# Seventy matmuls of zeros in the first chunks' TensorE waits, and a new order of the first list of steps

## The chip, the cores and the metric

The kernel runs on one core of one Trainium2 chip. The metric is the device time in microseconds (us) of one execution. TensorE multiplies matrices into PSUM, which has eight banks; VectorE (DVE), ScalarE (ACT) and GpSimd (POOL) do the elementwise work; SyncE (SP) issues all DMA transfers of this kernel. Each engine and the SP queue works through its own instructions in order and waits on semaphores for the others.

## The reference

Pooled attention, then two MLPs on its output (shapes: 4 batches, 8 heads, 576 tokens, head size 64; d_model 512; d_ff 1536 and 2048):

```python
k_p = k.reshape(B, H, Sp, 8, D).mean(axis=3)      # v_p likewise
scores = scale * np.matmul(q, k_p.transpose(0, 1, 3, 2))
attn = softmax(scores)                            # rows, with 1e-9 in the sum
x = heads_joined(np.matmul(attn, v_p))            # 2304 x 512
xn = x / sqrt(mean(x * x) + 1e-6) * rms_g
x = (silu(xn @ w_gate) * (xn @ w_val)) @ w_out    # first MLP
h = x @ w_in2
return silu(h) @ w_out2                           # second MLP
```

The MLPs' weights are float64 words in memory; the kernel converts them to float32 by integer operations on both halves of a word, and splits each float32 number into a high and a low part, so that three fast matmuls stand for one exact one.

## The kernel before, in words

The 2304 tokens are eight chunks of 288; two chunks make a batch of the attention. Everything the kernel does is cut into steps, and four long lists written out by hand (`start`, `pair`, `last`, `second`) say in which order the steps are issued. `play` reads a list: a token such as `1x0` means the next step of work `x` number 0 of chunk 1, and a suffix such as `:g` puts that step's free operation on POOL (`:v` on DVE, `:a` on ACT). Since every engine is in order, the list fixes the order on each engine; steps of different engines that stand beside each other in it don't hinder one another.

The steps that the change and the prediction touch, all from the first 60 us:

- `K`, `V`, `Q`: loads of a block of k, v or q (SP). The blocks of k and v first go to early slots, later to rotating buffers; the q blocks of chunks 1 and up share two buffers (`q_load`, lines 299 to 309), so 1Q3 has to wait until a block of chunk 1 was used by its scores.
- `B n`: one of 36 weight blocks, seven steps: load (SP), shift (DVE), scale (ACT), sign (ACT, or DVE with `:v`), join (DVE), high part (ACT), low part (POOL). Blocks 0, 1, 2 are gate, val and out number 0, blocks 3, 4, 5 number 1, and so on (`w_block`, line 207).
- `k j`: the sum over eight keys (DVE), then two copies into `kbd`, a block-diagonal tile whose other half stays zero (`k_sum`, line 331). `a i` and `d i` do the same for v into `vbd0` and `vr0`.
- `m j`: the scores of one pair of heads, three matmuls on TensorE, six records in the profile (line 405). `s j`: the negated maximum (DVE, line 416), then six exponentials with their sums and a scaling (ACT, line 423). `w j`: the reciprocal (DVE), the weighting (DVE or POOL) and a copy of the remaining columns to `rest`.
- `p i`: three transposes on TensorE (line 456) and a copy out of PSUM. `x j`: the product with v on TensorE (lines 490, 491, called `pv`), its square (ACT, line 498), its scaled copy to `xraw`, and, for chunk 0, the sums of squares as matmuls with one column (line 509, `x0.3` is the fourth step of x0).
- `r`, `n`: the root mean square, its broadcast by matmuls (`rs`, line 542) and its use. `y j`: the split of x into `xT`. `Z`: a store of x.
- `G f`, `H f`, `D f`: the gate, val and out matmuls of the first MLP for a chunk and a slice of d_ff, twelve matmuls each (lines 257 to 259).

Chunk 0's attention takes its PSUM banks from a rotation (`att_bank`, line 313) over the tags up (two banks), acc0 to acc3 and att (two banks); chunk 1 and later ones take att alone. A bank is taken again only when the engines that read it are done. The banks acc0 to acc3 hold the out sums of the first MLP from D0 on.

`setup` (line 99) and a memset of `kbd` (line 1065) run ahead of the lists. The tile `early_x` has 1024 columns, of which the first 864 are used.

Of the kernel before, what the change touches and what calls it, by code (L numbers as in the profile page):

```python
# [9 lines left out]
F32 = mybir.dt.float32  # L10
# [12 lines left out]
def tile_pooled_attention_then_two_mlps(  # L23
# [16 lines left out]
    nc = tc.nc  # L40
# [8 lines left out]
    P = 128  # L49
# [3 lines left out]
    CH = S // 2  # L53
# [45 lines left out]
    def setup():  # L99
        make_identity(nc, ident)  # L100
        nc.gpsimd.memset(ones, 1.0)
        nc.gpsimd.memset(mhalf, -0.5)

        nc.vector.tensor_reduce(
            out=mask, in_=ident.rearrange("p (q h r) -> p h q r", h=4, r=REST), axis=AX.XY, op=ALU.add
        )

        nc.gpsimd.memset(vbd0, 0.0)
        for e in range(2):
            nc.vector.tensor_copy(out=vbd[:, e], in_=kbd.rearrange("p j r -> p (j r)")[:, :NPAIR * P])  # L110
# [8 lines left out]
    def ring(dtype, name, n):  # L119
        return w_pools[n < NRING // 2].tile([P, 1024], dtype, tag="w", bufs=NRING // 2, name=name)  # L120
# [5 lines left out]
    early_x = ring(F32, "early_x", next(n_early))  # L126
    early_v = ring(F32, "early_v", next(n_early))
# [183 lines left out]
    banks = ["up", "up", "acc0", "acc1", "acc2", "acc3", "att", "att"]  # L311

    def att_bank(c, name):

        tag = "att"
        if c == 0:
            tag = banks.pop(0)
            banks.append(tag)
        return psum.tile([P, 512], F32, tag=tag, bufs=1 if tag.startswith("acc") else 2, name=name)

# [524 lines left out]
    x2 = {}  # L845
# [148 lines left out]
    def down2(c, m):  # L994
# [70 lines left out]
    nc.vector.memset(kbd, 0.0)  # L1065
# [41 lines left out]
    )  # L1107
    pair = (
# [246 lines left out]
```

## Time and profile before

| what | value |
|---|---|
| median of three runs | 922.28 us (917.54 to 922.48) |
| the profiled execution | 922.12 us, span 920.3 us |
| busy share of the span | PE 98%, DVE 69%, ACT 59%, POOL 41% |
| mean granted clock of TensorE | 0.981 of 2.4 GHz |
| the chain that ended last | PE 81%, DVE 9%, DMA 4%, POOL 3% |

The page of a profile gives shares and groups, the windows give busy times of a stretch, the timeline single instructions. Times count from the start of the span. PE is TensorE, PEld its weight loads. The granted clock is a share of 2.4 GHz and has two levels, 1.00 and 0.50. Matmuls overlap in the records, so their pace is read from the start of one to the start of the next rather than from their length. A wait is put down to the engine whose signal came last.

### The profile page before, as it was taken

The numbers are of one execution on the slowest core, as the hardware profiler recorded it, in microseconds if no ns is written. First come the engines' busy times: TensorE is split into PE (matmuls) and PEld (weight loads), VectorE is DVE, ScalarE is ACT, GpSimd is POOL, SyncE is SP. The second block draws the span as 40 slices with busy tenths as digits, with TensorE's granted clock in tenths as the row PEclk, the third lists the DMA queues.
The fourth block names the chain that finished last, engine by engine and source line by source line (L and its number), as shares of the span: only waits on it lengthen the run. The fifth ranks groups of instructions, "written<-read, shape, count | busy, mean of one in ns | idle before, by whom it ended". The sixth has DMA issues, their size and how long they took to land.

```text
span 920.3 us, 17356 instructions
## 1 busy us (share of the span) xinstructions
PE 901.8 (98%) x6122; PEld 875.4 (95%) x6122; DVE 631.2 (69%) x1254; ACT 542.5 (59%) x1453; POOL 375.8 (41%) x487
## 2 busy tenths in 40 slices
PE   5999999999999999999999999999999999999998
PEld 4689999999999999999999998999999999999998
DVE  6789988765554835443368779658986579766675
ACT  5688887364254714345444546677666677576653
POOL 6435443344215621200027746881038910388200
PEclk8589999999999999999999999999999999999999
DMA  8645642342215321244367885266862668614486
GB/s 281 204 140 174 218 134 64 120 152 78 62 41 134 116 66 40 84 137 144 131 230 258 291 280 182 89 206 206 269 213 63 213 187 264 233 49 161 125 263 208
DMA packets 85259, 149.79 MB, mean 163 GB/s; under 512 B 8627, under 2 KB 53812, under 8 KB 85172
## 3 DMA queue, kind: packets, MB, share of 16 engines
q1 hardware_dynamic: 85172, 148.68, 50.0%
q8 instruction: 48, 0.79, 0.4%
q14 instruction: 39, 0.32, 0.1%
HBM read 116.21 MB, written 32.44 MB: 162 GB/s over the span
## 4 chain that ended last, share of the span: by engine, by line
PE 81%; DVE 9%; DMA 4%; POOL 3%; issue 2%; ACT 1%; SPq 0%; ACTq 0%; POOLq 0%; DVEq 0%
PE P L773 38%; PE pv L257 4%; PE pv L259 4%; PE pv L258 4%; PE pg L258 4%; PE pg L257 4%; PE pg L259 4%; PE acc L258 4%; PE acc L257 4%; PE acc L259 4%; PE sc L405 2%; PE pT L456 1%; PE pv L491 1%; DMA out<-out2s 1%; DMA xw_raw<-xw 1%
## 5 line engine op out<-in xcount | busy, mean ns | idle before, releaser
L773 PE MATMUL P<-xP,in 128*128 128x384 f32 x1008 | 179.5, 338 | 0.7 <-POOL in L244 0.5
L773 PEld LDWEIGHTS P<-xP,in 128*128 128x128 f32 x1008 | 177.5, 188 | 1.6 <-POOL in L244 0.8
L773 PE MATMUL P<-out,hc 128*128 128x256 f32 x1512 | 172.7, 276 | 0.0
L773 PEld LDWEIGHTS P<-out,hc 128*128 128x128 f32 x1512 | 172.5, 188 | 0.0
L244 POOL TENSOR_TENSOR in<-in,in 128x256 fp32r<-128x256 f32 x96 | 78.8, 830 | 112.1 <-ACT in L237 64.5
L237 ACT ACTIVATE hc<-h 128x384 fp32r<-128x384 f32 x144 | 74.1, 525 | 41.8 <-PE P L773 37.7
L244 DVE TENSOR_TENSOR hc<-h,hc 128x384 fp32r<-128x384 f32 x144 | 81.6, 590 | 19.6 <-ACT hc L237 17.7
L257 PE MATMUL pg<-xT,w_gate 128*128 128x288 f32 x240 | 73.0, 304 | 0.8 <-DVE hT L244 0.8
L257 PE MATMUL pv<-xT,w_val 128*128 128x288 f32 x240 | 73.0, 304 | 0.1
L257 PE MATMUL acc<-hT,w_out 128*128 128x288 f32 x240 | 72.4, 302 | 0.0
L258 PE MATMUL pg<-xT,w_gate 128*128 128x288 f32 x240 | 71.6, 298 | 0.2
L258 PE MATMUL acc<-hT,w_out 128*128 128x288 f32 x240 | 71.2, 297 | 0.2 <-DVE hT L244 0.2
L259 PE MATMUL pg<-xT,w_gate 128*128 128x288 f32 x240 | 71.2, 297 | 0.0
L259 PE MATMUL pv<-xT,w_val 128*128 128x288 f32 x240 | 70.9, 295 | 0.0
L258 PE MATMUL pv<-xT,w_val 128*128 128x288 f32 x240 | 70.8, 295 | 0.0
L259 PE MATMUL acc<-hT,w_out 128*128 128x288 f32 x240 | 70.8, 295 | 0.0
L423 ACT ACTIVATE pr<-sc,mx 96x72 f32<-96x72 f32 x192 | 57.9, 314 | 17.8 <-DVE mx L416 17.8
L624 ACT ACTIVATE th<-pg 128x288 f32<-128x288 f32 x57 | 23.5, 413 | 72.1 <-PE pg L259 71.9
L244 POOL TENSOR_TENSOR in<-sums,in 128x256 fp32r<-128x256 f32 x72 | 59.0, 829 | 2.4 <-ACT in L237 2.0
L626 DVE SCALAR_TENSOR_TENSOR th<-th,pg 128x288 f32<-128x288 f32 x57 | 25.6, 448 | 40.1 <-ACT th L624 40.0
L257 PEld LDWEIGHTS pg<-xT,w_gate 128*128 128x128 f32 x240 | 45.7, 190 | 1.3 <-issue 1.0
L258 PEld LDWEIGHTS pg<-xT,w_gate 128*128 128x128 f32 x240 | 45.6, 190 | 0.6 <-DVE xT L244 0.6
(233 smaller groups left out, 2304.4 us busy)
## 6 DMA issues: line engine op xcount, KB each, us to landing
out<-out SPq DMA_DIRECT2D x84, 512.0 KB, 4.7
out<-out2s SPq DMA_DIRECT2D x56, 256.0 KB, 4.1
in<-in SPq DMA_DIRECT2D x24, 512.0 KB, 3.6
raw<-in_moe_w_out_dram SPq DMA_DIRECT2D x18, 512.0 KB, 4.5
raw<-in_moe_w_in_dram SPq DMA_DIRECT2D x16, 512.0 KB, 3.7
early_raw<-in_moe_w_gate_dram SPq DMA_DIRECT2D x10, 512.0 KB, 4.2
early_raw<-in_moe_w_val_dram SPq DMA_DIRECT2D x10, 512.0 KB, 4.9
early_raw<-in_moe_w_out_dram SPq DMA_DIRECT2D x10, 512.0 KB, 4.8
```

What stands on the lines that cost most here:

```text
L237: nc.scalar.activation(out=out, in_=in_, func=AF.Copy, scale=1.0 if scale is None else scale)
L244: ENGINES[engine[0] or usual].tensor_tensor(out=out, in0=in0, in1=in1, op=op)
L257: nc.tensor.matmul(ps, lhsT=whi, rhs=xhi, start=first, stop=False)
L258: nc.tensor.matmul(ps, lhsT=whi, rhs=xlo, start=False, stop=False)
L259: nc.tensor.matmul(ps, lhsT=wlo, rhs=xhi, start=False, stop=last)
L405: nc.tensor.matmul(ps[:TT, a * 2 * SP:(a + 1) * 2 * SP], lhsT=qT[:, a * TT:(a + 1) * TT], rhs=kbd[:, j, :], start=True, stop=True,)
L423: nc.scalar.activation(out=pr[:, a, e], in_=s4[:, a, e], func=AF.Exp, bias=mx[:, a, e:e + 1], accum_out=sm[:, a, e],)
L456: nc.tensor.transpose(ps[:n, a * TT:(a + 1) * TT], src, ident[:TT, :TT])
L491: nc.tensor.matmul(ps, lhsT=vr0[:RR, j, :], rhs=pT_t[c, NPAIR + j // 2], start=False, stop=True)
L624: nc.scalar.activation(out=th, in_=pg, func=AF.Tanh, scale=0.5)
L626: nc.vector.scalar_tensor_tensor(out=th, in0=th, scalar=1.0, in1=pg, op0=ALU.add, op1=ALU.mult)
L773: nc.tensor.matmul(ps, lhsT=a, rhs=b, start=first and n == 0, stop=n == 2, skip_group_check=True)
```

## The change

A step `T` (`warm`) is added to the lists' vocabulary: one float32 matmul of a 128x128 block of zeros with itself, into a PSUM tile `idle` that nobody reads. The zeros are columns of `early_x` that were free; DVE sets them first of all in `setup`, ahead of `kbd`. `idle` takes the bank acc3, so chunk 0's rotation has seven banks instead of eight.

```diff
     def setup():
+        nc.vector.memset(zero, 0.0)
+        nc.vector.memset(kbd, 0.0)
         make_identity(nc, ident)
...
     early_x = ring(F32, "early_x", next(n_early))
+    zero = early_x[:, 3 * CH:3 * CH + P]
...
-    banks = ["up", "up", "acc0", "acc1", "acc2", "acc3", "att", "att"]
+    banks = ["up", "up", "acc0", "acc1", "acc2", "att", "att"]
...
+    idle = []
+
+    def warm(n):
+
+        if not idle:
+            idle.append(psum.tile([P, 512], F32, tag="acc3", bufs=1, name="idle"))
+        nc.tensor.matmul(idle[0][:, :P], lhsT=zero, rhs=zero, start=True, stop=True, skip_group_check=True)
+        yield
...
-    nc.vector.memset(kbd, 0.0)
     setup()
...
     start = (
-        "B0 K1 Q1 K0 k1 Q0 V4 V5 k1:g k0 K2 m1 k0:g 1Q0 1Q1 K3 a5 s1 a4:v V0 m0 Q2 B0 B0 s1 V3 d4:g Q3 B0:v g0 "
-        "1m1 B1 B2 1m0 k2 k2:g s0 s0 1Q2 w1 B0 1s1 w1:g d5:g w1:g a0:v a0:g m2 1s1 w0 p1 k3 w0:g p0 s2 s2 1w1 "
...
+        "K1 T13 T12 T11 T10 T9 T8 T7 T6 T5 Q1 K0 k1 B0 V4 V5 Q0 k1:g k0 K2 T4 m1 T3 T2 T1 T0 T56 1Q1 k0:g T55 s1 "
+        "1Q0 K3 m0 a5 V0 Q2 B0 B0 s1 V3 a4:v d4:g Q3 B0:v T54 T53 1m1 B1 1m0 k2 k2:g s0 s0 w1 w1:g 1Q2 B0 1s1 "
...
-             "X": x2_steps, "O": turn, "g": lambda n: g_load()}
+             "X": x2_steps, "O": turn, "g": lambda n: g_load(), "T": warm}
```

All seventy T steps are in `start`. Read from the two lists, TensorE's order up to G1 becomes (Tn is n fillers in a row; x0.3 is the squares' sum of x0; r0 is the broadcast `rs`):

```
before: m1 m0 1m1 1m0 m2 p1 p0 m3 p4 1p1 p2 x0 1m2 1p0 x1 1m3 x0.3 p3 p5 1p4 x3 x2 1x1
        x3.3 x1.3 2m0 1p3 x2.3 1x0 1p5 G0 1p2 r0 1x2 1x3 H0 2p0 G1
after:  T10 m1 T6 m0 T2 1m1 1m0 T5 m2 p1 T7 m3 p0 T8 1p1 T2 p4 p2 1m2 T6 x0 1p0 x1 x0.3 p3
        1m3 T3 p5 T6 1p4 T5 x3 x2 1x1 x3.3 x1.3 2m0 1p3 x2.3 T7 1x0 1p5 G0 1p2 r0 T3 1x3
        1x2 H0 2p0 G1
```

The loads begin with B0 K1 Q1 K0 Q0 V4 V5 before and K1 Q1 K0 B0 V4 V5 Q0 after; later B4 2K0 B3 V2 1Q3 2K1 becomes V2 2K0 B4 1Q3 B3 2K1. On POOL the order w1 d5 w1 a0 w0 k3 becomes w1 w0 w1 k3 d5 (then, behind two more steps, a0). On DVE the work up to G0 is nearly the same: B7's shift moves ahead of it, two steps of B8 and B4 behind it. `pair`, `last` and `second` hold the same steps as before in an order changed in many places, mostly by one to three places on an engine; of the wide gates 8G9 moves back by 21 places on TensorE and 9G5 forward by 11. Two operations change their engine: the high part of B27 (ACT to DVE) and a copy of 6w2 (DVE to POOL).

## Rows read from the trace of the kernel before

**Rows 1.** The page, parts 1 and 2: busy time, then the span in 40 slices.

```profile
PE 901.8 (98%) x6122; PEld 875.4 (95%) x6122; DVE 631.2 (69%) x1254; ACT 542.5 (59%) x1453; POOL 375.8 (41%) x487
...
PEclk8589999999999999999999999999999999999999
...
GB/s 281 204 140 174 218 134 64 120 152 78 62 41 134 116 66 40 84 137 144 131 230 258 291 280 182 89 206 206 269 213 63 213 187 264 233 49 161 125 263 208
```

**Rows 2.** Windows: length; PE, PEld, DVE, ACT, POOL busy (count); clock; DMA share; GB/s.

```profile
13.40:16.80 3.40, 1.44 (x9) 1.02 (x9) 3.10 (x6) 3.37 (x23) 3.12 (x8) 1.00 1.05 381
16.80:21.60 4.80, 2.98 (x12) 2.21 (x12) 2.59 (x9) 4.71 (x30) 4.55 (x6) 0.50 0.79 268
21.60:48.50 26.90, 26.85 (x90) 17.61 (x91) 20.06 (x43) 17.80 (x77) 13.74 (x20) 0.50 0.56 177
48.50:51.20 2.70, 2.70 (x14) 2.70 (x13) 1.61 (x4) 2.52 (x5) 0.66 (x1) 0.55 0.06 25
```

**Rows 3.** Timeline of TensorE: start, length, line, operation, operands, count, idle before, releaser.

```profile
7.26 3.19 PE L405 MATMUL sc<-kbd,early 128*96 128x144 f32 x12 [7.26 <-POOL kbd L241]
...
14.45 0.98 PE L405 MATMUL sc<-kbd,early 128*96 128x144 f32 x6 [1.12 <-POOL kbd L241]
...
17.63 0.74 PE L456 MATMUL pT<-ident,pr 96*128 96x96 f32 x3 [1.72 <-POOL pr L244]
18.87 1.75 PE L405 MATMUL sc<-kbd,early 128*96 128x144 f32 x6 [0.50 <-POOL kbd L241]
...
21.65 1.22 PE L456 MATMUL pT<-ident,pr 96*128 96x96 f32 x6 [0.54 <-DVE early_pT L239]
```

**Rows 4.** Windows: the stretch with the low clock and the one behind it.

```profile
10.00:60.00 50.00, 46.11 (x195) 33.68 (x195) 38.38 (x84) 37.58 (x161) 26.55 (x40) 0.66 0.60 195
60.00:120.00 60.00, 58.79 (x436) 56.31 (x435) 58.73 (x133) 51.20 (x155) 30.62 (x39) 1.00 0.62 195
```

**Rows 5.** Timeline of TensorE again, around and behind the clock's rise.

```profile
35.81 1.33 PE L490 MATMUL pv<-early_pT,early_v 128*128 128x288 f32 x2
...
38.33 1.33 PE L490 MATMUL pv<-pT,early_v 128*128 128x288 f32 x2
...
45.66 1.31 PE L490 MATMUL pv<-pT,early_v 128*128 128x288 f32 x2
...
51.52 0.83 PE L542 MATMUL rs<-ident,ms 96*128 96x96 f32 x6
52.24 0.75 PE L490 MATMUL pv<-pT,early_v 128*128 128x288 f32 x2
...
53.60 0.75 PE L490 MATMUL pv<-pT,early_v 128*128 128x288 f32 x2
...
58.54 0.90 PE L405 MATMUL sc<-kbd,qT 128*96 128x144 f32 x6
59.27 0.59 PE L528 MATMUL ms<-ones,sq 128*96 128x1 f32 x6
```

**Rows 6.** Timeline of DVE: its first instruction.

```profile
0.91 0.54 DVE L1065 MEMSET kbd<- 128x576 f32 x1 [0.91 <-PEq L1339]
```

**Rows 7.** The chain that ended last, its first steps: start, length, what.

```profile
1.22 4.26 DMA early<-in_k_dram
...
6.35 0.40 POOL kbd L241
```

**Rows 8.** Timeline of the SP queue: DMA issues.

```profile
0.72 0.45 SPq L155 DMA_DIRECT2D early_raw<-in_moe_w_gate_dram  x1
...
15.24 0.50 SPq L283 DMA_DIRECT2D kv<-in_v_dram  x1
26.85 0.33 SPq L307 DMA_DIRECT2D qT<-in_q_dram  x1
```

**Rows 9.** Timeline of ACT: first exponentials of two successive readings.

```profile
13.07 0.32 ACT L423 ACTIVATE pr<-sc,mx 96x72 f32<-96x72 f32 x1 [1.23 <-DVE mx L416]
...
15.12 0.30 ACT L423 ACTIVATE pr<-sc,mx 96x72 f32<-96x72 f32 x1
```

328 rows, old and new, of tables (last, pair, second, start) are left out of this document.

## The prediction

> **What bounds the kernel now.** I read the page's busy shares first: TensorE (PE) is busy for 98% of the span, so only what shortens PE's own work or its waits can shorten the run, and the PEclk row has a dip to 5 tenths in its second slice [rows 1]. The windows cut where the clock changes show what that dip is: from 16.8 us to about 51 the granted clock is 0.50, which is 1.2 GHz, and elsewhere 1.00, which is 2.4 GHz [rows 1, 2]. Two things are to be seen there. First, between 21.6 and 48.5 PE is busy for 26.85 of 26.90 us, so at half clock PE itself is the bound; no engine beside it is over 75% busy. Secondly, a busy PE was not enough to bring the clock back. It fell after 13.4 to 16.8, in which PE worked only 1.44 of 3.40 us, and rose within 48.5 to 51.2, when the dense `pg` matmuls of G0 came; between them stand short scores, transposes and the 32-row `pv` products.
>
> The PE timeline adds something that the clock rows hide [rows 3]. Twelve score records take 3.19 us at 7.26, or 0.266 each, and six take 1.75 at 18.87, under a recorded clock of 0.50; but six take 0.98 at 14.45. So the first scores also ran at 1.2 GHz, although the windows print no fall there: the dense scores from 7.26 to 13.33 lifted the clock, and the gaps behind them lost it. The same rows give the gaps: 7.26 before the first score, then 1.12, 1.72, 0.50 and 0.54, for POOL's and DVE's operands.
>
> After 60 us things are different: PE 58.79 and DVE 58.73 of 60 us [rows 4]. There DVE is as full as PE, so time won earlier stays won only if DVE arrives earlier by as much. From 10 to 60 DVE is busy for 38.38 of 50, so it has 11.6 us of idle time to give.
>
> **What a filler costs.** Each T step is one fp32 matmul, 128x128 by 128 columns, in two records as the other fp32 matmuls have. None is in the trace, so bounds from start to start at full clock: the `rs` records (weights 128 columns wide, 96 moving) come every 0.72/6 = 0.12 us, so 0.24 a filler; the scores every 0.73/6 = 0.122 for 144 columns, by columns 0.22 a filler; the `pv` products every 1.36/4 = 0.34 for 288 columns, by columns 0.30 a filler [rows 5]. I take 0.24, since `rs` has the same weights and nearly the same length; both ends stay for the range.
>
> **The change part by part.** All is counted against the `rs` products behind G0, at 51.52 [rows 5], since the order behind them is nearly the same.
>
> 1. Ten fillers ahead of the first score. They need only the small memset of `zero`, which now runs ahead of the 0.54 us memset of `kbd` [rows 6], so PE can begin at about 1.1 us. At half clock (0.48 each) they end at 5.9. The first score is late today because of k1: its load takes 4.26 us from 1.22 on, and DVE's sum and POOL's two copies, the first at 6.35, follow it [rows 7]. In the new list K1 takes B0's place at the head of SP, 0.5 us earlier (0.72 against 1.22) [rows 7, 8], and B0's 512 KB no longer run ahead of it, 1.9 us at the 281 GB/s of the first slice [rows 1]. So k1 is earlier by 0.5 to 1.9 us, and the fillers let the score start no earlier than 5.9: between -0.5 and -1.4, taken as **-1.4**, since the load is nearer to its bytes than to its place in the queue. B0 moves behind K1, Q1 and K0; its first step on DVE stands behind the first maximum, which hides it.
>
> 2. The clock. Work at 1.2 GHz today is 6.1 us of scores (7.26 to 13.33) and 16.8 to 51.0 less 1.9 of gaps, 32.3: together 38.4. At 2.4 GHz a score goes from 1.75 to 0.90 and a `pv` product from 2.52 to 1.36 start to start [rows 3, 5], a factor near 0.53, so the gain is 38.4 x 0.47 = **-18.0** if the clock is held from the first score on.
>
> 3. The gaps of 1.12, 1.72, 0.50 and 0.54 [rows 3] become room for fillers: **-3.9**, to be set against the next item.
>
> 4. The fillers between the first score and G0 are 57: 6, 2, 5, 7, 8, 2, 6, 3, 6, 5, 7 in their groups. 57 x 0.24 = **+13.7** (12.5 to 17.1). Three more ahead of 1x3 add **+0.7**.
>
> 5. New waits: **+2.9** (0 to 5). Chunk 0 now rotates over seven PSUM banks, not eight, so p0 takes a bank of the pair "att" that chunk 1 shares, and 1p1, 1m3, 1p4 and 1x0 each wait until ACT has read the scores in the bank they need. One such reading, of six exponentials and their sums, holds ACT from 13.07 to 15.12, 2.05 us [rows 9]. ACT has nine of these before 1x0, 18.5 us, with copies and conversions between them, and with PE at double speed it has few gaps left. Following the new order by hand with the row durations, these four wait about 0.7, 0.9, 1.0 and 0.3. DVE and POOL queue behind: s3, 1s3 and 2s0 on DVE can't start before their scores.
>
> 6. The SP queue gains, with nothing added. Today the load 1Q3 blocks SP from 15.7 to 26.85, because its buffer is freed by the scores 1m2, at the end of that wait [rows 8]; everything behind it (2K1, B6, 2K3, B7) waits. In the new list 1m2 stands ahead of x0 and comes some 5 us earlier, and V2, 2K0 and B4 are ahead of 1Q3. Only B3 falls behind 1Q3; with 1m2 at 21 its data land near 25.5, where DVE asks for them. I count this at nothing: it keeps DVE's input ahead of a faster PE, and costs about as much as PE would win if it failed (rival 1).
>
> 7. The rest. On PE no step of the first list moves by more than three places among the real steps. In the other lists a few wide gates move further (8G9 by 21), where PE has no idle time. B27's copy goes from ACT to DVE and one copy of 6w2 from DVE to POOL, each under 1 us and far from G0. I take 0, between -2 and +2.
>
> Sum: -1.4 - 18.0 - 3.9 + 13.7 + 0.7 + 2.9 = -6.0. The profiled execution took 922.12 against a span of 920.3 and a median of 922.28 in the runs, so 922.12 - 6.0 = **916.1**, span and what lies around it alike.
>
> **A rule to weigh.** In 21.6 to 48.5 PE had no gaps and stayed at 1.2 GHz [rows 2]. The Trainium skill, in "TensorE: Matmul & The Clock Gate", section "Why this matters for your kernels", says that keeping TensorE continuously busy releases the clock; the rows here disagree, since busy time of this kind did not. By that rule the fillers would matter only in the gaps. The same page, Part 4 on transposes, says that transposes don't count as busy in the same way; that fits the stretch, and makes rivals 2 and 3 possible.
>
> **The rivals.**
> 1. *The other engines become the bound.* With PE twice as fast, the stretch is a chain of maximum (DVE), exponentials (ACT), weighting (POOL, DVE), transposes and copies. For it: ACT and DVE are 75 to 77% busy in 10 to 60 [rows 4]. Against it: a gain of 6 needs half of DVE's 11.6 idle. New waits of 5 rather than 2.9, with fillers at 0.30 each (+3.4), leave a gain of 0.5; half of both leaves 3.3, 918.8. Taken at 919.
> 2. *The clock is lifted but lost again* in the one long stretch without fillers, x3 to x2's square sums. It is 9.85 us today from x2's product at 35.81 to 45.66, and 2.5 more with x3's [rows 5], so 12.4 at half and 6.5 at full clock: losing it gives back about 5.8. That is 922, no change. For it: exactly this work left the clock low. Against it: at full clock `rs` and two `pv` products in a row left it up, since the second came 1.36 behind the first and the scores at 58.54 again took 0.90 [rows 5].
> 3. *Zeros don't count, and the run is slower.* If the clock takes no notice of matmuls of zeros, PE stays at half clock to G0, and 57 fillers at 0.48 are 27.4 us, of which 3.9 fall into gaps, and 1.4 come back from the earlier start; the last three cost 1.4: +23.5, which is 945 (21 to 31 more with fillers at twice 0.22 and twice 0.30). It decides at one point: whether the clock stands at 1.00 when x0 comes. Against it: the scores lifted the clock at about 13 us, although half of their moving operand `kbd` is zeros. The same page of the Trainium skill (Part 1) says that all-zero operands don't trip the current limiter, so one throttle there does see the data; no run here shows that for this one.
> 4. *The later lists cost more than they bring* (item 7, or DVE full from 60 us on): 924 to 926.
>
> **How the numbers follow.** Forecast 0.58, rival 1 0.17, rival 2 0.12, rival 3 0.08, rival 4 0.05. The low end is fillers at 0.22 and no new waits, some 10 us, so 911 with a us for item 7; the high end takes in rivals 1 and 2: 922. Outside it are rivals 3 and 4 and small tails, 0.2 in all. With 0.5% (4.6 us, about what a measurement of this kernel can tell from no change), faster is the forecast, 0.58; same is rival 1 and most of rival 2, 0.27; slower is rivals 3 and 4 and the rest of 2, 0.15.
>
> **What would show it.** The clock at 1.00 from about 7 us through 44; six score records in 0.9 us from the second score on; fillers 0.24 apart; the `rs` products near 44.8 (51.52 before); ACT or DVE named in the waits ahead of 1p1, 1m3 and 1p4; 1Q3 issued near 21; and the same lead of about 6 us still there at 120 and at the end. Wrong would be: a clock of 0.50 anywhere from 15 to 44 for more than a few us (rivals 2, 3), PE gaps of over 5 us in sum before G0 (rival 1), or a lead that shrinks from G0 to the end (rival 4).

## The result, and the profile after

The changed kernel takes 910.33 us (median; 908.33 to 911.95), the kernel before beside it on the same chip 922.38: a ratio of 0.9878, with a 95% interval of 0.9856 to 0.990. In a second comparison it took 911.21 against 921.72 (0.9885, 0.987 to 0.990). The forecast was 916.1 and the range 911 to 922: the direction and the mechanism came out, the gain is twice the forecast, and the first median lies 0.7 us below the range. The profiled execution took 909.87 with a span of 908.1.

The page of the changed kernel, parts 1 and 2, beside [rows 1]:

```profile
PE 899.4 (99%) x6262; PEld 882.0 (97%) x6262; DVE 628.3 (69%) x1255; ACT 540.0 (59%) x1452; POOL 382.7 (42%) x488
...
PEclk9999999999999999999999999999999999999999
```

TensorE has 140 records more (70 fillers of two) and is busy 2.4 us less, since the dip to 5 tenths in the second slice is gone. The windows of the changed kernel, cut where its clock changes, then the two stretches of [rows 4] (columns as in [rows 2]):

```profile
6.48:26.96 20.48, 18.82 (x147) 16.41 (x146) 17.01 (x34) 16.89 (x95) 17.75 (x26) 1.00 0.88 282
26.96:30.37 3.41, 3.41 (x18) 3.33 (x17) 2.63 (x8) 2.33 (x11) 3.35 (x5) 0.50 0.85 249
30.37:42.56 12.19, 12.19 (x85) 9.10 (x85) 10.54 (x23) 9.35 (x40) 5.69 (x10) 1.00 0.83 260
10.00:60.00 50.00, 49.12 (x348) 41.71 (x347) 44.28 (x96) 42.13 (x187) 32.65 (x45) 0.97 0.72 228
60.00:120.00 60.00, 59.58 (x452) 58.55 (x452) 57.84 (x133) 52.03 (x148) 31.97 (x39) 1.00 0.65 211
```

From 6.48 us on the clock stands at 2.4 GHz but for 3.41 us, where it was at 1.2 GHz for 34 us before. DVE, 38.38 of 50 us busy in [rows 4], is now at 44.28: it does the same work in a shorter stage. The timeline of TensorE in the changed kernel, against [rows 3] and [rows 5] (L330 is the filler, L417 the scores, L554 `rs`):

```profile
1.03 4.63 PE L330 MATMUL idle<-early_x 128*128 128x128 f32 x20 [1.03 <-DVE early_x L100]
5.46 1.40 PE L417 MATMUL sc<-kbd,early 128*96 128x144 f32 x6
6.70 1.50 PE L330 MATMUL idle<-early_x 128*128 128x128 f32 x12
9.32 0.95 PE L417 MATMUL sc<-kbd,early 128*96 128x144 f32 x6 [1.11 <-DMA early<-in_q_dram]
...
13.83 0.98 PE L417 MATMUL sc<-kbd,early 128*96 128x144 f32 x6 [0.54 <-POOL kbd L244]
...
17.85 1.98 PE L330 MATMUL idle<-early_x 128*128 128x128 f32 x16
19.67 0.41 PE L468 MATMUL pT<-ident,pr 96*128 96x96 f32 x3
...
26.88 1.56 PE L417 MATMUL sc<-kbd,qT 128*96 128x144 f32 x6
...
44.49 0.83 PE L554 MATMUL rs<-ident,ms 96*128 96x96 f32 x6
```

The first score starts at 5.46 (7.26 before). Ten fillers take 4.43 us at half clock, 0.443 each; eight take 17.85 to 19.67 at full clock, 0.2275 each. No gap stands at 1p1, 1m3, 1p4 or 1x0, where I expected waits for a bank. `rs` starts at 44.49, 7.03 ahead of its 51.52 before.

Below, the lead of a step is its start in the trace of before less its start in the other trace (e1 to e11 are the runs of the sections that follow). What matters is where it grows:

| lead, us | before starts | changed | e1 | e2 | e3 | e4 | e11 |
|---|---|---|---|---|---|---|---|
| `rs` behind G0 | 51.52 | 7.0 | 8.4 | 0.4 | 1.0 | 1.5 | 7.6 |
| H0 | 54.96 | 6.5 | 7.8 | -0.2 | 0.6 | 0.6 | 7.0 |
| first gate of chunk 2 (2G0) | 109.67 | 7.6 | 8.9 | -0.1 | 1.5 | 1.4 | 8.1 |
| first gate of chunk 6 (6G0) | 357.7 | 8.8 | 9.6 | 0.1 | 2.7 | 1.4 | 8.5 |
| first wide product (aW0) | 625.0 | 11.7 | 8.6 | 3.8 | 5.5 | 1.3 | 12.3 |
| last product (cW55) | 915.4 | 12.3 | 8.6 | 3.8 | 5.6 | 1.3 | 12.6 |

So 7 of the 12 us come from the first 45, as the steps of the prediction had it (6.7), and 5 more behind them, where I had put nothing. Each column is one execution. In e12, another execution of the changed kernel, the lead was 5.7 at `rs`, 5.2 at H0 and 11.1 at the last product: the first stage differs by 1.3 us, the growth behind H0 is the same (5.9, and 5.8 above).

### The profile page after: what moved, and what is told of

The parts are those of the page before. It is cut to its first block, busy times and chain, and to the rows that moved or that the text cites. A ratio compares the mean times of both kernels' runs of the same rounds, so it can differ in the third digit from the quotient of the medians.

```text
span 908.1 us, 17610 instructions
## 1 busy us (share of the span) xinstructions
PE 899.4 (99%) x6262; PEld 882.0 (97%) x6262; DVE 628.3 (69%) x1255; ACT 540.0 (59%) x1452; POOL 382.7 (42%) x488
## 4 chain that ended last, share of the span: by engine, by line
PE 87%; DVE 5%; DMA 4%; ACT 2%; issue 1%; POOL 1%; SPq 1%; ACTq 0%; DVEq 0%; POOLq 0%
PE P L785 38%; PE pv L260 5%; PE pv L261 5%; PE pv L262 5%; PE pg L260 5%; PE acc L260 4%; PE acc L261 4%; PE pg L261 4%; PE pg L262 4%; PE acc L262 4%; PE sc L417 2%; DMA out<-out2s 2%; PE pT L468 1%; PE idle L330 1%; DMA early<-in_v_dram 1%
## 5 line engine op out<-in xcount | busy, mean ns | idle before, releaser
L262 PEld LDWEIGHTS pv<-xT,w_val 128*128 128x128 f32 x240 | 45.3, 189 | 0.6 <-POOL w_val L247 0.6
L260 PEld LDWEIGHTS pv<-xT,w_val 128*128 128x128 f32 x240 | 45.1, 188 | 0.7 <-ACT kbd L240 0.4
```

Of the source, the lines that this page charges most:

```text
L260: nc.tensor.matmul(ps, lhsT=whi, rhs=xhi, start=first, stop=False)
L262: nc.tensor.matmul(ps, lhsT=wlo, rhs=xhi, start=False, stop=last)
```

## Which part pays: the lists apart

Theory: the new order and the fillers of the first list bring about 6 us, the later lists the rest. Rival: the first list brings all, and the lead grows later because every engine comes early.

**e1**, the new first list with the old later ones.

```diff
     pair = (
-        "2Y1:v 4V5 2Y0:a 3G0 4a5 4V4 I0 3H0 3G0 3G0 4Q1 3G1 2Y2:a 3H0 3H0:v 3G1 3H1 4K1 3H0:v 2Y0 4Q0 3G1 2Y3:v "
+        "2Y1:v 4V5 2Y0:a 3G0 4K1 4a5 I0 3G0 3G0 3H0 4Q1 3G1 2Y2:a 3H0 3H0:v 3G1 3H0:v 3H1 I0 2Y0 2Y3:v 3G1 4K0 "
...
```

> The changed kernel's first list with its seventy fillers, in front of the three later lists of before. Theory S (the two halves are worth their gains separately): only the lead of the first stage remains, 6.5 to 7 us, so about 915.5, with the old stalls back (PE idle of about 1 us near 545 and 0.7 near 557). Theory L (the later gain came from arriving earlier, so that DVE, ACT and DMA run ahead and stalls vanish by themselves): the whole 12 us, about 910.5.

Measured: 914.79, ratio 0.9931 (0.9911 to 0.9951), against 921.27 before. **e2**, the other half: the kernel before with the new `pair`, `last` and `second`.

```diff
     pair = (
-        "2Y1:v 4V5 2Y0:a 3G0 4K1 4a5 I0 3G0 3G0 3H0 4Q1 3G1 2Y2:a 3H0 3H0:v 3G1 3H0:v 3H1 I0 2Y0 2Y3:v 3G1 4K0 "
+        "2Y1:v 4V5 2Y0:a 3G0 4a5 4V4 I0 3H0 3G0 3G0 4Q1 3G1 2Y2:a 3H0 3H0:v 3G1 3H1 4K1 3H0:v 2Y0 4Q0 3G1 2Y3:v "
...
```

> The three later lists of the changed kernel behind the first list of before, no filler, eight banks, TensorE at half clock from 17 to 51 us as before. Theory S: the later lists alone bring 5 to 5.7 us, about 917. Theory L: nothing, 922, since nothing arrives earlier.

Measured: 917.5, ratio 0.9965 (0.9949 to 0.9982). The two halves are 6.5 and 3.8 us, together 10.3 of the 11 to 12: the theory stands, and the rival's 922 for e2 doesn't. The waits of TensorE from 350 to 625 us show a part of what the later lists take away. First before, then e1, then e2, then the changed kernel (what waited, for what: us, times, longest):

```profile
PE acc L258 <- DVE hw L244: 0.8, 1, 0.8
PE P L773 <- POOL in L244: 0.5, 1, 0.5
PE acc L257 <- ACT hw L237: 0.2, 1, 0.2
PE P L773 <- ACT in L237: 0.2, 1, 0.2
PE pg L258 <- DVE xw L244: 0.2, 1, 0.2
```

```profile
PE pg L260 <- ACT xw L240: 1.3, 1, 1.3
PE acc L261 <- DVE hw L247: 0.8, 1, 0.8
PE acc L260 <- ACT hw L240: 0.6, 1, 0.6
PE P L785 <- POOL in L247: 0.5, 1, 0.5
...
```

```profile
PE pg L257 <- ACT thw L803: 0.2, 1, 0.2
```

```profile
PE pg L260 <- ACT thw L815: 0.9, 1, 0.9
```

The old lists leave 1.9 us of waits in this stretch, 3.6 when the first list hands over earlier (e1: its lead shrinks there from 9.6 to 8.6), and the new lists 0.2 behind the old first list and 0.9 behind the new one. The early start alone is partly given back to these waits.

**e11** asks which later list it is: the changed kernel with only `pair` of before. Its lists divide a few steps differently, so the second steps of 6k3, 6a0 and 6a1, which copy three sums over keys and values of chunk 6 into their tiles, are left out, and 5G0, 4Y0 and 4Y1 begin in `pair` already.

```diff
     pair = (
-        "2Y1:v 4V5 2Y0:a 3G0 4a5 4V4 I0 3H0 3G0 3G0 4Q1 3G1 2Y2:a 3H0 3H0:v 3G1 3H1 4K1 3H0:v 2Y0 4Q0 3G1 2Y3:v "
+        "2Y1:v 4V5 2Y0:a 3G0 4K1 4a5 I0 3G0 3G0 3H0 4Q1 3G1 2Y2:a 3H0 3H0:v 3G1 3H0:v 3H1 I0 2Y0 2Y3:v 3G1 4K0 "
...
```

> The changed kernel with the list `pair` of the kernel before; `last` and `second` are the new ones. In the traces of e1 (old later lists) and of the changed kernel the lead grows alike from 100 to 350 us, and differs from 350 to 620 us, where `last` runs: so `last` brings the 4 us and `pair` nothing, and this kernel is within 1 us of the changed one, 909.5 to 911.5. Rival: `pair` hands on a better state to `last`: 912 to 914.5, towards e1 (914.8).

Measured: 910.53, ratio 0.9872 (0.9855 to 0.9888), the changed kernel beside it 911.21. (Three executions took 909.54 to 910.59; a fourth took 2284, which nothing here explains.) `pair` brings nothing; the lead grows from 8.5 to 12.3 between 6G0 and aW0, in `last` (e11 has the new `second` too, but from aW0 to the end its lead grows by 0.3 only). Of those 3.8 us, the waits above name 1.9: in e11 no wait is listed from 350 to 625. The rest lies in steps that each take some tenths less without a wait being named (the first wide gate 2.35 us in the changed kernel rather than 3.24, of which 0.2 is the wait for xw above), and its cause stays open.

## Fillers and order, each alone

Theory: the fillers are what holds the clock, whatever the order. Rival: each without the other is worth little.

**e3**, the changed kernel without its fillers.

```diff
     start = (
-        "K1 T13 T12 T11 T10 T9 T8 T7 T6 T5 Q1 K0 k1 B0 V4 V5 Q0 k1:g k0 K2 T4 m1 T3 T2 T1 T0 T56 1Q1 k0:g T55 s1 "
+        "K1 Q1 K0 k1 B0 V4 V5 Q0 k1:g k0 K2 m1 1Q1 k0:g s1 1Q0 K3 m0 a5 V0 Q2 B0 B0 s1 V3 a4:v d4:g Q3 B0:v 1m1 "
...
```

> The changed kernel without the seventy T steps; new order, seven banks, new later lists. If the fillers hold the clock: it is at 0.50 from before 20 us to G0 again, the rs products behind G0 come between 48 and 52 instead of 44.5, and the whole lands 4 to 7 us over the changed kernel, 914.5 to 917.5. Rival (the new order is what matters and the denser order holds the clock by itself): within 2 us of the changed kernel, about 911, with the clock at 1.00.

Measured: 916.39, ratio 0.9953 (0.9935 to 0.9971). The windows, cut at its clock:

```profile
14.10:20.90 6.80, 3.29 (x25) 2.51 (x24) 5.32 (x12) 6.37 (x42) 6.50 (x10) 1.00 0.97 313
20.90:24.30 3.40, 3.40 (x15) 2.64 (x14) 3.29 (x8) 3.12 (x17) 3.34 (x4) 0.50 0.14 42
24.30:31.20 6.90, 4.62 (x30) 2.87 (x30) 6.04 (x13) 6.64 (x32) 6.54 (x11) 0.99 0.98 322
31.20:51.60 20.40, 19.73 (x66) 13.66 (x67) 13.74 (x30) 9.68 (x34) 6.92 (x9) 0.50 0.48 158
```

The clock rises, falls, rises and falls again, the last time for 20 us with TensorE busy. The fillers hold it, and are worth 5 to 6 us in this order (916.39 less 911.21 or 910.33). **e4**, the same seventy fillers ahead of the same steps, with seven banks, in the old order.

```diff
     start = (
-        "B0 K1 Q1 K0 k1 Q0 V4 V5 k1:g k0 K2 m1 k0:g 1Q0 1Q1 K3 a5 s1 a4:v V0 m0 Q2 B0 B0 s1 V3 d4:g Q3 B0:v g0 "
+        "B0 K1 Q1 K0 k1 Q0 V4 V5 k1:g k0 K2 T0 T1 T2 T3 T4 T5 T6 T7 T8 T9 m1 k0:g 1Q0 1Q1 K3 a5 s1 a4:v V0 T10 "
...
```

> Before with the seventy fillers alone, put ahead of the same TensorE steps as in the changed kernel; old order of all lists, old order of the loads, seven banks. If the clock is the cause: it is at 1.00 for most of 7 to 45 us and the rs products come 4 to 6 us earlier than 51.5, so 916 to 918.5. Rival (fillers cost what the clock brings, and the gain came from the order, above all 1m2 ahead of x0 and the load 1Q3 behind it): 921 to 923.

Measured: 921.69, ratio 1.0011 (0.9991 to 1.003): no change, so my expectation failed and the rival's time came out. The windows at its clock, its waits in the first 60 us, and its first score:

```profile
6.20:30.10 23.90, 20.39 (x158) 17.81 (x158) 18.07 (x39) 18.05 (x102) 21.32 (x32) 1.00 0.75 244
30.10:33.50 3.40, 3.40 (x19) 3.32 (x18) 2.88 (x7) 2.26 (x14) 3.29 (x3) 0.50 0.94 273
33.50:40.34 6.84, 6.84 (x42) 4.52 (x42) 4.52 (x8) 3.19 (x11) 2.84 (x5) 1.00 0.94 339
40.34:47.16 6.82, 6.82 (x31) 6.08 (x30) 5.52 (x14) 4.59 (x19) 2.28 (x3) 0.50 0.35 102
```

```profile
PE sc L417 <- POOL kbd L244: 2.2, 3, 1.2
PE idle L330 <- DVE early_x L100: 1.0, 1, 1.0
PE sc L417 <- DMA qT<-in_q_dram: 0.9, 1, 0.9
PE pT L468 <- ACT pr L435: 0.9, 1, 0.9
```

```profile
6.87 0.98 PE L417 MATMUL sc<-kbd,early 128*96 128x144 f32 x6 [1.20 <-POOL kbd L244]
```

Of the 3.9 us of waits behind the first filler, 1.2 stand ahead of the first score and 2.7 behind it. The old gaps behind it were 3.9 [rows 3], and the changed kernel has 1.7 left ahead of G0. So in the old order the fillers take the place of little more than 1 us of waits, and 10.2 us stay at half clock, where 3.4 do in the changed kernel behind its first score. By the prediction's factors: (38.4 - 10.2) x 0.47 = 13.3 back, 60 x 0.2275 = 13.7 paid, and the waits and the first score, 0.4 earlier, bring 1.6 more. That is a gain of 1.2, against a lead of 0.6 at H0 in its trace and none in the median of ten executions. Alone, the fillers bring 0 (e4) and the order about 1.1 (e3 against e2, whose intervals overlap, so it may be nothing); together 6.5 (e1).

## How many fillers, and where

**e5** leaves out every second filler, **e6** all behind the first score (ten stay), **e10** puts each twice.

```diff
-        "K1 T13 T12 T11 T10 T9 T8 T7 T6 T5 Q1 K0 k1 B0 V4 V5 Q0 k1:g k0 K2 T4 m1 T3 T2 T1 T0 T56 1Q1 k0:g T55 s1 "
+        "K1 T13 T11 T9 T7 T5 Q1 K0 k1 B0 V4 V5 Q0 k1:g k0 K2 m1 T3 T1 T56 1Q1 k0:g s1 1Q0 K3 m0 a5 V0 Q2 B0 B0 s1 "
...
-        "K1 T13 T12 T11 T10 T9 T8 T7 T6 T5 Q1 K0 k1 B0 V4 V5 Q0 k1:g k0 K2 T4 m1 T3 T2 T1 T0 T56 1Q1 k0:g T55 s1 "
+        "K1 T13 T12 T11 T10 T9 T8 T7 T6 T5 Q1 K0 k1 B0 V4 V5 Q0 k1:g k0 K2 T4 m1 1Q1 k0:g s1 1Q0 K3 m0 a5 V0 Q2 "
...
-        "K1 T13 T12 T11 T10 T9 T8 T7 T6 T5 Q1 K0 k1 B0 V4 V5 Q0 k1:g k0 K2 T4 m1 T3 T2 T1 T0 T56 1Q1 k0:g T55 s1 "
+        "K1 T13 T70 T12 T71 T11 T72 T10 T73 T9 T74 T8 T75 T7 T76 T6 T77 T5 T78 Q1 K0 k1 B0 V4 V5 Q0 k1:g k0 K2 T4 "
...
```

> The changed kernel with every second filler left out (35 of 70 stay, some in every group). Theory 'few are enough': the clock stays at 1.00 as it did with seventy; the 35 that are gone free at most 35 x 0.23 = 8 us on TensorE, but DVE was at work for 44.28 of the 50 us from 10 to 60 and its y2 ended 0.08 us before G0, so most of it turns into waits: within 1.5 us of the changed kernel, 909 to 911. Theory 'the number counts': the clock falls again in the stretches behind the first scores for 10 to 25 us, and the time is 913 to 916.5, between the changed kernel and the one without fillers (916.4).

> The changed kernel with only the first ten fillers and T4 (ahead of the first scores); the 59 behind the first score are left out. Theory 'the early lift does it': with the clock at 1.00 from the first score on, the dense stretch keeps it, and the time is 909 to 911.5. Theory 'the later fillers hold it': the clock falls in the gaps behind the first scores as in the kernel before (where it had come up at 13.4 and was lost at 16.8), and the time is that of the kernel without fillers less the early lift of 1 to 2 us: 914 to 916.5.

> The changed kernel with every filler twice, 140. The clock stays at 1.00. By my fourth term all of a filler lies on the path: 70 more, ten of them ahead of the first score at 0.44 each (4.4) and 60 at 0.2275 (13.7), less the 1.9 us of waits that are left ahead of G0: about +16, 926. Rival: DVE is nearly the bound of this stage (44.28 of 50 us), TensorE's fillers lie partly in the time that it would wait for DVE's operands, and they cost half or less: 916 to 919.

Measured: e5 913.84, ratio 0.9922 (0.9898 to 0.9946); e6 916.91, ratio 0.9964 (0.9948 to 0.9979); e10 924.23, ratio 1.0031 (1.0018 to 1.0044). In e5 the number counts: its clock was at 1.2 GHz from 26.58 to 33.40 and from 40.23 to 47.06. In e6 the early lift is worth nothing (e3, with no filler, 916.39). Its windows:

```profile
6.57:9.99 3.42, 0.98 (x8) 0.77 (x7) 2.29 (x5) 1.65 (x8) 1.65 (x3) 1.00 1.05 301
9.99:13.40 3.41, 3.41 (x15) 2.91 (x13) 3.41 (x7) 2.55 (x18) 3.11 (x6) 0.50 1.03 364
13.40:16.81 3.41, 1.75 (x11) 1.16 (x11) 2.98 (x8) 3.06 (x21) 3.08 (x7) 1.00 1.05 329
16.81:54.36 37.55, 34.64 (x123) 24.06 (x124) 24.79 (x55) 23.05 (x104) 18.85 (x26) 0.50 0.54 180
```

Each time that TensorE had worked little (0.98 of 3.42 us, 1.75 of 3.41), the clock fell next. From 10 to 60 us in e10:

```profile
10.00:60.00 50.00, 50.00 (x380) 45.34 (x379) 34.19 (x71) 30.62 (x146) 24.92 (x36) 0.93 0.57 182
```

With 140 fillers TensorE doesn't wait in these 50 us. The second seventy cost 13.0 us beside the changed kernel of the same comparison (924.23 - 911.21), where 16 was expected. With the 1.9 us of waits in the first 60 that they fill, that is 14.9 / 70 = 0.21 each, close to the 0.2275 of a filler at full clock. The ten ahead of the first score cost less than expected: it starts at 8.04, 2.6 later than in the changed kernel rather than 4.4, since the clock rose at 6.18, among the fillers. So fillers lie on the path; the first seventy pay because the clock gives back more.

**e7** moves four of the six fillers ahead of x0 behind x1, into the stretch after which the clock fell in the profile above; **e9** does this, moves three of the five ahead of x3 to 2m0, and has the loads of e8.

```diff
-        "s3 B1:v V2 1w0 B2 p2 p4:v a1:v 1p1 p1 2K0 B2 s3 a1 1m2 1w1:g 1w0:g p2:v T36 T35 T34 T33 T32 T63 B4 1Q3 "
-        "B3 B1 a3 2K1 x0 B6 x0 1p0 x1 w3 x0 w3:g w2:v B0:g 1s2 1p0 2K3 B7 w3:g a2:v 1w0 x0 2k0 B3 B4 p3 1m3 B0 "
+        "V2 1w0 B2 p2 p4:v a1:v 1p1 p1 2K0 B2 s3 a1 1m2 1w1:g 1w0:g p2:v T36 T35 B4 1Q3 B3 B1 a3 2K1 x0 B6 x0 1p0 "
+        "x1 T34 T33 T32 T63 w3 x0 w3:g w2:v B0:g 1s2 1p0 2K3 B7 w3:g a2:v 1w0 x0 2k0 B3 B4 p3 1m3 B0 1s2 1s3 B2:v "
...
```

> The changed kernel with four of the six fillers ahead of x0 moved behind x0 and the first half of x1, into the stretch from 23 to 27 us after which the clock fell to 0.50 for 3.4 us. If the fall came from that stretch having no fillers, the clock stays at 1.00 there and the time is 1 to 2 us shorter: 908.3 to 909.5. Rival: the fall comes and goes by itself, or the gain is taken by waits for DVE: within 0.7 us of the changed kernel.

> The same seventy fillers, spread: four of the six ahead of x0 stand behind x1 (as in e7), three of the five ahead of x3 stand behind x3 and x2, ahead of 2m0; and the loads B0 and Q0 are at the head of the queue again (as in e8). The single falls of the clock came at 27 us (changed kernel), at 36 (e8) and none in the profile of e7, each in a stretch without fillers. If spreading them takes these falls away in nearly every execution, the granted clock is 0.998 or more in all runs and the median falls to the level that the best executions of the changed kernel, e7 and e8 showed, 908.3 to 909.0. Rival: a fall comes somewhere in some executions all the same, or waits take the gain: 910 to 911.5, as the changed kernel beside it.

Measured: e7 911.41, ratio 0.991 (0.9875 to 0.9945); e9 913.02, ratio 0.9896 (0.9879 to 0.9912), against 911.21 for the changed kernel beside it. In both the theory fell. The profiled execution of e7 had no fall of the clock in this stage, but another had a mean clock of 0.993 and took 915.04; e9's profile has two falls, from 27.21 to 34.04 and from 40.87 to 47.70. Neither beats the changed kernel. **e12**, the changed kernel once more, shows why the first profile misled me.

> The changed kernel itself once more, beside the three others on the same chip: 909 to 911.5, with a fall of the clock in most executions. It tells whether its time and its clock go together from execution to execution: a granted clock lower by 0.001 is 0.9 us more at half clock, and should be about 0.5 to 0.9 us more time.

Measured: 911.21, ratio 0.9885 (0.987 to 0.990). Its windows ahead of the fall (the second is the last part of the first) and in it, then TensorE around the fall:

```profile
4.90:35.62 30.72, 28.78 (x213) 23.92 (x212) 25.73 (x52) 23.51 (x122) 24.56 (x37) 1.00 0.92 294
20.00:35.62 15.62, 15.59 (x104) 11.43 (x102) 14.45 (x31) 12.64 (x57) 13.44 (x19) 1.00 0.80 257
35.62:42.45 6.83, 6.83 (x37) 6.82 (x37) 5.67 (x16) 4.99 (x20) 2.73 (x3) 0.50 0.68 214
```

```profile
34.98 1.54 PE L521 MATMUL ms<-ones,sq 128*96 128x1 f32 x12
36.37 1.73 PE L417 MATMUL sc<-kbd,qT 128*96 128x144 f32 x6
...
39.25 3.33 PE L330 MATMUL idle<-early_x 128*128 128x128 f32 x14
42.38 0.69 PE L502 MATMUL pv<-pT,early_v 128*128 128x288 f32 x2
```

The same instructions kept the clock at 27 us, where it fell the first time, and lost it at 35.6, within the square sums of x3 and x1, behind the `pv` products of x3, x2 and 1x1; seven fillers then took 3.33 us, where they had taken 1.81 in the first profile. The lead fell from 6.4 at 2m0 (36.37) to 3.3 at 1x0 (42.38), nearly all of it the price of this fall, by the prediction's factor 6.83 x 0.47 = 3.2. How much is lost differs from execution to execution: e7 took 908.58, 910.01, 912.81 and 915.04 at mean clocks of 0.999, 0.999, 0.996 and 0.993; e8 908.27 to 911.90 at 0.999 to 0.996; the changed kernel in its first comparison 908.33 to 911.95 at 0.999 to 0.994. That is 0.7 to 1.2 us for 0.001. My expectation mis-stated this: 0.001 of 909 us is 1.8 us at half clock, of which 0.47, 0.85 us, is lost. The four executions of e12 itself all had 0.996, so they say nothing on it.

## The first loads

**e8** tests the first term of the sum: B0 and Q0 go back to the head of the queue.

```diff
-        "K1 T13 T12 T11 T10 T9 T8 T7 T6 T5 Q1 K0 k1 B0 V4 V5 Q0 k1:g k0 K2 T4 m1 T3 T2 T1 T0 T56 1Q1 k0:g T55 s1 "
+        "B0 K1 T13 T12 T11 T10 T9 T8 T7 T6 T5 Q1 K0 Q0 k1 V4 V5 k1:g k0 K2 T4 m1 T3 T2 T1 T0 T56 1Q1 k0:g T55 s1 "
...
```

> The changed kernel with the loads B0 and Q0 at their old places at the head of the SP queue (B0 K1 Q1 K0 Q0). My first term says that K1 at the head brings the first score forward by 1.4 us: so up to 1.4 us slower, first score at 6.0 to 6.9. Rival: the 1.80 us that the first score won were half given back when m0 waited 1.11 us for Q0, which had been moved behind B0; with Q0 early again m0 does not wait, and the time is within 0.5 us of the changed kernel.

Measured: 910.48, ratio 0.9884 (0.9858 to 0.9911): the rival. The first steps of TensorE in e8:

```profile
6.88 0.98 PE L417 MATMUL sc<-kbd,early 128*96 128x144 f32 x6 [1.26 <-POOL kbd L244]
7.69 1.50 PE L330 MATMUL idle<-early_x 128*128 128x128 f32 x12
9.03 0.90 PE L417 MATMUL sc<-kbd,early 128*96 128x144 f32 x6
```

The first score is 1.42 later than in the changed kernel, but m0 doesn't wait for Q0 and starts 0.29 earlier. What the new order of the loads won at m1 it lost at m0.

## Why the prediction was right, and where not

1. *Ten fillers and the first loads, -1.4.* The first score came 1.80 earlier. But the step looked at B0 behind K1 and not at Q0, which was moved behind B0 as well: m0 waited 1.11 us for it (1.8 in e12), and e8 shows no gain from the new place of the loads. Worth about 0, not 1.4.
2. *The clock, -18.0.* Right in kind, 2.0 too large. Behind the first ten fillers 1.0 us at the first score's start and 3.41 us later stayed at half clock, so the term came to -(38.4 - 4.4) x 0.47 = -16.0; in e1, with no fall, all of it.
3. *Gaps, -3.9,* and 5. *bank waits, +2.9.* The gaps became room for fillers. The four bank waits cost nothing: 1p1, 1m3, 1p4 and 1x0 started at 19.67, 26.88, 31.55 and 41.10, each right behind the step ahead of it. I had let them wait until ACT was through with the bank; by the order in which the banks are taken, all four started 1.0 to 1.2 us into a reading whose six exponentials last 1.8. The last exponentials of 1s0 and 1s2, whose banks 1p1 and 1m3 take:

```profile
20.02 0.32 ACT L435 ACTIVATE pr<-sc,mx 96x72 f32<-96x72 f32 x1
...
27.28 0.33 ACT L435 ACTIVATE pr<-sc,mx 96x72 f32<-96x72 f32 x1
```

   In place of these waits came 1.11 and 0.54 us of others (Q0 and POOL's `kbd`): +1.7.
4. *Fillers, +13.7 and +0.7.* 57 x 0.2275 = 13.0, and 0.7: near, and e10 shows that they lie on the path.
6. *The SP queue, 0.* 1Q3 was issued at 22.02, as expected near 21, and TensorE waited for none of the loads behind it.

The sum of 1 to 6 for the changed trace is -1.8 - 16.0 - 3.9 + 13.7 + 1.7 = -6.3, against 6.0 forecast and a lead of 6.5 at H0; e1, which is these items and the rest of the first list, measured 6.5. That the sum comes so close to the forecast is in part luck: the clock gave back 2.0 less, and the earlier first score, the fillers' price and the waits made up 2.3.

7. *The rest of the lists, 0 between -2 and +2.* **This is the term that was mis-sized.** The later lists measured 3.8 alone (e2) and 3.6 to 4.5 on top of the first list (914.79 less 911.21 or 910.33): `last` holds nearly all (e11 and its lead). Between H0 and 6G0, mostly in the rest of `start`, the lead grows by 1.5 to 2.3 us with the new order of that list (changed kernel, e1, e3, e11) and by 0.3 to 0.8 with the old one (e2, e4). I dismissed these lists since TensorE has no idle time there. But a busy share near 100% was no floor. From H0 to the end, first before, then the changed kernel:

```profile
54.96:920.30 865.34, 858.00 (x5959) 844.07 (x5958) 593.31 (x1174) 506.97 (x1299) 347.57 (x437) 1.00 0.50 160
48.47:908.10 859.63, 853.67 (x5959) 843.34 (x5958) 589.06 (x1173) 505.45 (x1300) 351.31 (x438) 1.00 0.49 161
```

   The stretch is 5.7 us shorter with the same 5959 records at the same clock. TensorE's idle time falls by 1.4 of this (7.3 to 6.0), its busy time by 4.3: most of what was won had stood in the rows as work. What made the same records take longer is not shown. I had put a price on each wait of the first 60 us and on nothing behind them.

The rivals: *1, other engines become the bound*, came close: DVE ended xT at 42.64, 0.08 us behind G0's start at 42.56. But G0 didn't wait for it; the one wait for DVE up to 60 us behind the first filler is that of a later gate, G2, 0.27 us at 56.06. *2, the clock lost in a stretch without fillers*, took place in part, at x0 to p3 in one execution and at the place named in another, for 1.6 to 3.2 us rather than 5.8. *3, zeros don't count*, fell: in e12 the clock rose at 4.90, when TensorE had done nothing but fillers. *4, the later lists cost*, went the other way.

## What to carry over

A busy stretch at half clock was won here with extra matmuls, but only in an order made for them, with fewer waits beside them and less time at half clock (e4). Alone the fillers were worth nothing and the order about 1 us; together they were worth 6.5. When a change rewrites an order everywhere, don't take a busy share near 100% for a floor: here 4 us were won some tenths at a time where TensorE was over 98% busy, and more of it in busy time than in waits.

## What the runs showed that I had not expected

Matmuls of zeros lift the clock alone (e12, 4.90 us). Being busy by the profile doesn't keep it: in e12 TensorE was at work for 15.59 of the 15.62 us from 20 us to the fall, and all through the fall. The Trainium skill, in "TensorE: Matmul & The Clock Gate", section "Why this matters for your kernels", tells to keep TensorE busy without long gaps so as to hold the clock; these rows disagree, as [rows 2] did. What stood right ahead of both falls of the changed kernel were `pv` products and square sums with one column, in the first trace with transposes between them. Whether the same instructions lost the clock differed between executions, and what decides it stays open.
